# A fused attention and MLP kernel: first projections by row pieces of the q, k weights, products of chunk 0 in halves, weights of chunk 1 spread by SBUF to SBUF transfers

## The chip, the cores and the metric

The kernel runs on one core of one Trainium2 chip. The metric is the device time of one execution in microseconds (us); the time before is the median of three runs. One more execution was profiled, and all views are of that one.

## The reference, cut to what matters

```python
S, D, H, Dh, W, dil, F = 2048, 512, 32, 16, 8, 2, 1376      # batch 1, bf16

def attention(x, wqkv, wo):                                  # x: layernormed rows
    q, k, v = split(x @ wqkv)                                # 32 heads of 16 each
    idx = pos[:, None] - arange(W)[None, :] * dil            # 8 keys per row: 0, 2, ..., 14 rows back
    logits = einsum("bhsd,bhswd->bhsw", q, k[idx]) * Dh ** -0.5
    attn = softmax(where(idx >= 0, logits, -1e9))
    return einsum("bhsw,bhswd->bhsd", attn, v[idx]) @ wo

def mlp(x, W_gate, W_up, W_down):
    gate = relu(x @ W_gate)
    return (gate * (x @ W_up)) @ W_down

h  = x + attention(layernorm(x), wqkv, wo)
h2 = h + mlp(layernorm(h), W_gate, W_up, W_down)
```

## The kernel before

The 2048 rows are taken in four chunks of 512 (`tk` = 0 to 3). Each chunk passes through the same stages, and the stages of different chunks are interleaved.

1. **Layernorm and transposition.** DVE takes row statistics (L431, L434), ACT the reciprocal root (L444, L448), DVE writes the normed rows (L466). They are transposed by TensorE (L495) and copied out of PSUM by ACT or DVE (L511, L509), or, for those named in `DMAT`, by DMA transposes on SP's queue (L484). All of chunk 3's first layernorm goes by DMA (`xtd`).
2. **Projections.** Twelve of 512 columns each (L536): four each of q, k and v, every one of them four matmuls, one for each of four row blocks (`dt`) of the weights. ACT copies each out (L544). The first four of chunk 0 are run in two halves of the chunk's rows, 256 columns at a time.
3. **Scores.** DVE multiplies q by the shifted k (L583, `pr`), for four shifts and two of the four dimension groups at a time, 128x4096 elements in one instruction. TensorE sums over the head's dimensions (L589, `sc`), ACT takes the exponential (L619); in chunk 0 DVE masks the first columns (L622, `mk`). TensorE and ACT form one over the softmax sum (L639, L642, L645).
4. **Spreading the weights.** Each weight is needed in four partitions. In chunks 0 and 1 TensorE does that (L689, `bc`, two groups of four matmuls of 32x512 that run beside each other), and ACT copies eight results out (L695, `be`). In chunks 2 and 3 (`BCD`) eight transfers of 128 KB from SBUF to SBUF on SP's queue do it (L679, `bd`). In chunks 1 to 3 the weights are scaled by the reciprocal first (L663, `am`).
5. **Weights times v.** DVE multiplies (L710, `mu`, 128x4096, once for each of four dimension groups) and adds up eight products: first eight to four, by an accumulating DMA that GpSimd issues (L742, `ta`, 512 KB, chunks 0 to 2) or on DVE, then four to two and two to one on DVE (L713, L717, L736).
6. **Output projection and MLP.** L762 and L765 (`wo`), the residual (L771, L773), the second layernorm, the up and gate projections (L800), their copies on ACT (L804, L807), the product on DVE (L820), the down projection (L837, `dn`), the sum (L848) and the store (L854).

**What sets the order.** Each step is an `Op` with an engine, an expected duration, its dependencies and its buffers. `Plan.order` plays all of them through, with one queue for each engine that is sorted by the table `RANK`, and the program is written out in the order of the planned start times. So the order on each engine is fixed when the program is built, and an instruction that waits holds up all that stand behind it on its engine. The expected load times (`xload`, `wload`) and durations only shape that order and the choice of buffers; the chip waits for semaphores.

At the start each of SP's and ACT's queues issues two x row blocks and two row blocks of the q, k weights:

```python
for j in range(BPC):
    (nc.scalar if j % 2 else nc.sync).dma_start(x_sm[:, j:j + 1, :], x_rows[:, j:j + 1, :])
for dt in range(NT):
    (nc.scalar if dt % 2 else nc.sync).dma_start(wqk_sb[:, dt:dt + 1, :], w3_r[:, dt:dt + 1, 0:2 * D])
nc.sync.dma_start(x_sm[:, BPC:2 * BPC, :], x_rows[:, BPC:2 * BPC, :])
```

While they land, TensorE runs 44 matmuls of zeros (L385), and 16 more behind its first transposes (L393).

Of the kernel before, what the change touches and what calls it, by code (L numbers as in the profile page):

```python
# [18 lines left out]
    0, 1, 2, 3, 4, 5, 6, 7, 8, 9, 10, 11, 12, 13, 14, 15, 16, 18, 19, 21,  # L19
    24, 32, 27, 17, 20, 22, 25, 26, 30, 35, 36, 29, 34, 37, 39, 41, 43, 47, 23, 28,  # L20
    31, 33, 38, 45, 48, 42, 59, 65, 40, 51, 55, 46, 56, 60, 49, 52, 57, 73, 76, 61,
    79, 67, 72, 71, 74, 80, 106, 88, 95, 75, 96, 91, 104, 103, 93, 113, 119, 127, 70, 85,
    94, 98, 102, 172, 175, 185, 130, 134, 136, 149, 152, 105, 108, 110, 114, 111, 188, 197, 223, 226,
    231, 179, 190, 217, 221, 228, 171, 180, 208, 211, 219, 158, 169, 195, 207, 210, 245, 252, 236, 241,
    239, 244, 243, 249, 256, 260, 247, 253, 246, 250, 255, 261, 266, 269, 276, 281, 275, 279, 285, 278,
    283, 282, 286, 291, 310, 315, 326, 330, 293, 322, 314, 324, 348, 329, 361, 337, 345, 339, 342, 346,
    350, 365, 333, 358, 349, 354, 340, 352, 353, 356, 363, 323, 328, 316, 321, 302, 313, 308, 312, 332,
    364, 373, 366, 370, 306, 379, 369, 394, 405, 359, 393, 355, 380, 402, 404, 421, 442, 445, 395, 424,
    453, 574, 374, 413, 447, 450, 389, 409, 436, 473, 50, 53, 44, 62, 54, 64, 58, 63, 66, 69,
    77, 90, 78, 83, 92, 81, 87, 82, 86, 89, 118, 129, 157, 170, 124, 196, 164, 178, 97, 101,  # L30
    166, 182, 100, 116, 150, 159, 132, 186, 107, 176, 137, 156, 109, 126, 200, 213, 218, 237, 232, 240,
    251, 258, 262, 264, 274, 284, 287, 288, 296, 294, 292, 298, 300, 307, 305, 309, 303, 318, 327, 360,
    367, 311, 319, 341, 347, 336, 343, 372, 377, 325, 334, 368, 375, 382, 385, 384, 388, 381, 383, 386,
    398, 390, 392, 397, 400, 387, 396, 401, 403, 406, 407, 408, 411, 414, 417, 410, 418, 412, 419, 422,
    457, 467, 434, 484, 477, 480, 461, 481, 491, 472, 475, 429, 466, 449, 460, 441, 476, 478, 433, 435,
    454, 458, 446, 451, 439, 443, 462, 474, 503, 427, 431, 469, 486, 502, 505, 508, 493, 512, 465, 525,
    507, 518, 511, 521, 529, 497, 516, 504, 513, 520, 531, 552, 569, 572, 524, 541, 666, 707, 514, 533,
    537, 540, 536, 539, 580, 708, 112, 120, 99, 121, 68, 84, 115, 122, 125, 133, 144, 163, 147, 160,
    165, 142, 148, 135, 145, 161, 229, 234, 233, 242, 187, 202, 177, 199, 174, 183, 192, 194, 184, 189,
    206, 235, 212, 215, 181, 191, 193, 205, 214, 238, 289, 265, 297, 317, 248, 257, 290, 301, 331, 335,  # L40
    338, 357, 344, 362, 371, 415, 425, 456, 459, 423, 432, 464, 470, 430, 438, 468, 471, 391, 399, 448,
    455, 479, 483, 490, 495, 485, 492, 482, 488, 487, 489, 499, 501, 494, 496, 498, 506, 509, 515, 519,
    522, 526, 528, 527, 534, 517, 532, 596, 601, 562, 594, 565, 589, 558, 591, 604, 544, 553, 542, 551,
    555, 560, 548, 550, 570, 549, 557, 546, 556, 579, 583, 568, 573, 586, 599, 608, 609, 614, 571, 576,
    603, 611, 618, 617, 626, 613, 629, 588, 631, 606, 627, 632, 620, 624, 585, 616, 635, 639, 662, 668,
    672, 623, 641, 643, 677, 628, 636, 638, 675, 634, 637, 645, 647, 117, 141, 128, 139, 131, 140, 123,
    138, 143, 146, 155, 162, 153, 167, 168, 173, 151, 154, 204, 225, 254, 268, 273, 299, 259, 270, 209,
    227, 216, 220, 267, 280, 224, 230, 201, 222, 198, 203, 263, 272, 271, 277, 304, 295, 320, 376, 378,
    351, 416, 420, 426, 428, 437, 444, 440, 463, 452, 530, 535, 543, 561, 500, 510, 523, 566, 547, 554,
    564, 567, 538, 545, 559, 563, 593, 597, 575, 578, 577, 581, 582, 587, 600, 602, 590, 598, 584, 595,  # L50
    592, 605, 607, 610, 619, 622, 615, 625, 621, 633, 612, 630, 657, 689, 683, 687, 667, 673, 671, 680,
    692, 640, 656, 658, 660, 648, 654, 650, 661, 664, 676, 679, 644, 652, 678, 682, 655, 663, 684, 649,
    651, 653, 670, 642, 646, 665, 669, 674, 694, 696, 685, 693, 659, 690, 681, 686, 698, 691, 699, 688,
    697, 701, 710, 714, 717, 719, 705, 709, 711, 715, 695, 702, 704, 706, 700, 703, 712, 713, 716, 718,
    720, 721,
# [36 lines left out]
class Plan:  # L92
# [23 lines left out]
    def order(self):  # L116
# [14 lines left out]
        while left:  # L131
# [36 lines left out]
            op.start, op.done = t, t + op.dur + op.lat  # L168
            if op.dq:
                at = max(t + op.dur + op.dq[0], free.get("DQ", 0.0)) + op.dq[1]  # L170
                free["DQ"] = at
                op.done = at + op.lat
            free[op.eng] = t + op.dur
# [18 lines left out]
def kernel(  # L192
# [22 lines left out]
    BCD = {(2,0):"SSSS",(2,1):"SSSS",(3,0):"SSSS",(3,1):"SSSS"}  # L215
    PRE = ()
    NAB = 0
# [127 lines left out]
    DAL = 5.5  # L345
    TDD, TDL = 1.25, 1.5
# [13 lines left out]
    HG = ([[0, 1, 2, 3]],) * 4  # L360

# [12 lines left out]
    def load(t):  # L374
        return add(None, "LD", 0.0, None, lat=t)

    xload = [[load(t) for t in (3.5, 3.7, 4.1, 4.35)]] + [[load(t)] * BPC for t in (9.15, 13.2, 15.4)]
    wload = {n: load(t) for n, t in
             (("q", 7.78), ("k", 7.78), ("v", 10.6), ("o", 17.1), ("u", 20.5), ("g", 24.0), ("d", 28.5))}
# [139 lines left out]
    for tk in range(NCK):  # L519
# [10 lines left out]
        for n, (c, t) in enumerate(seq):  # L530
# [3 lines left out]
            def f_mm(lo=0, hi=CS, c=c, t=t, mm=mm, xnT=xnT):  # L534
                for dt in range(NT):
                    nc.tensor.matmul(mm.t[:, lo:hi], lhsT=wv_sb[:, dt, t:D:NT] if c == 2 else wqk_sb[:, dt, c * D + t:(c + 1) * D:NT],  # L536
                                     rhs=xnT.t[:, dt, lo:hi], start=(dt == 0), stop=(dt == NT - 1))
# [9 lines left out]
            if tk == 0 and n < 4:  # L547

                a = None
                for i, (lo, hi, evs) in enumerate(((0, 2 * P, xev[0:2]), (2 * P, CS, xev[2:]))):  # L550
                    a = add(("qk%s%d" % ("ac"[i], n), tk), "PE", 4 * MM * (hi - lo) / CS + 0.02,
                            lambda f=f_mm, lo=lo, hi=hi: f(lo, hi), evs + [wl, a, fills[-1]], pr - 5, take=[mm],
                            use=[xnT], lat=PEL if i == 1 else 0.0)
            else:
                a = add(("qkv%d" % n, tk), "PE", 4 * MM, f_mm, xev + [wl], pr, take=[mm], use=[xnT], lat=PEL)
# [13 lines left out]
        for hf in range(2):  # L569
            sc, ex = Buf(at_s), Buf(ex_s)  # L570
            scd, prd = [], []
            for t in range(0, NT, 2):
# [13 lines left out]
                def f_sc(t=t, sc=sc, pb=pb):  # L586
                    for u in range(2):
# [5 lines left out]
                a = add(("pr%d" % hf, tk), "DVE", D40, f_pr, [d[k] for k in (t, t + 1) for d in (qd, kd, kp)],  # L593
                        apr, take=[pb], use=[qT], lat=DL)
                prd.append((a, pb, f_sc))
            if (tk, hf) in PRE:
# [72 lines left out]
        for w0 in range(0, W, BCN):  # L669
            hf = w0 // 4  # L670
            if (tk, hf) in BCD:
                for eng, q in (("SP", nc.sync), ("ACT", nc.scalar), ("POOL", nc.gpsimd)):
# [4 lines left out]
                    def f_bd(ws=ws, q=q, w0=w0, ab=ab, ex=exs[hf]):  # L677
                        for w in ws:
# [3 lines left out]
                                   take=[ab], use=[exs[hf]], lat=0.77, dq=(0.75 - 0.5 * (len(ws) - 1), 0.5 * len(ws))))  # L682
# [19 lines left out]
        for t in range(NT):  # L702
# [13 lines left out]
            def f_om(t=t, mt=mt, rc=rc, OT=OT):  # L716
                V.tensor_tensor(out=OT.t[:, t, :], in0=mt.t[:, 0, :], in1=rc.t[:], op=ALU.mult)  # L717

            m = add(("mu%d" % t, tk), "DVE", D40, f_mu, abd + [vd[t], kdone.get(("v", tk - 1, t))], tpr,
                    take=[mt], use=[ab], lat=DL)  # L720
# [17 lines left out]
            for n, du in ((4, D20), (2, D10), (1, D2)):  # L738
                f = lambda n=n, mt=mt, f=f_a: f(n, mt)
                if n == 4 and (tk, t) in DACC:  # L740
                    def f_da(mt=mt):
                        nc.gpsimd.dma_start(mt.t[:, 0:4, :], mt.t[:, 4:8, :], accum_op=ALU.add)  # L742

                    m = add(("ta%d" % t, tk), "POOL", 1.0, f_da, [m], tpr, use=[mt], lat=1.1, dq=(0.75, 2.74))
                    continue
                if n == 1 and tk in EARLY:
                    oev[t] = add(("tree%d" % t, tk), "DVE", du, f_al, [m], tpr, take=[OT], use=[mt], lat=DL)
                else:
                    m = add(("tree%d" % t, tk), "DVE", du, f, [m], tpr, use=[mt], lat=0.11)
# [39 lines left out]
        for f0 in range(0, NFT, 2):  # L789
# [3 lines left out]
            for ft in fts:  # L793
# [4 lines left out]
                def f_mm(w_sb, mm, ft=ft, fs=fs, hnT=hnT):  # L798
                    for dt in range(NT):
                        nc.tensor.matmul(mm.t[:fs, :], lhsT=w_sb[:, dt, ft * P: ft * P + fs],  # L800
                                         rhs=hnT.t[:, dt, :], start=(dt == 0), stop=(dt == NT - 1))
# [4 lines left out]
                def f_ge(gm=gm, gr=gr, fs=fs, i=ft - f0):  # L806
                    nc.scalar.activation(out=gr.t[:fs, i, :], in_=gm.t[:fs, :], func=ACT.Relu)  # L807

                a = add(("mm%d" % (f0 // 2), tk), "PE", 4 * MM, lambda f=f_mm, um=um: f(wu_sb, um), hev + [wload["u"]], pr,
                        take=[um], use=[hnT], lat=PEL)  # L810
                b = add(("ue%d" % (f0 // 2), tk), "ACT", A5, f_ue, [a], pr - 200, take=[ub], use=[um], lat=AL)
                c = add(("mm%d" % (f0 // 2), tk), "PE", 4 * MM, lambda f=f_mm, gm=gm: f(wg_sb, gm), hev + [wload["g"]], pr,
                        take=[gm], use=[hnT], lat=PEL)
# [93 lines left out]
```

## Time and profile before

| what | us |
|---|---|
| median of three runs (lowest, highest) | 200.46 (199.8, 200.73) |
| the profiled execution | 201.23 |
| its span, first to last instruction | 199.5 |
| TensorE (PE) busy | 191.6 (96%) |
| VectorE (DVE) busy | 152.6 (77%) |
| ScalarE (ACT) busy | 115.0 (58%) |
| GpSimd (POOL) busy | 12.6 (6%) |

The span leaves out 1.73 us of the profiled execution, ahead of the first instruction and behind the last. PE is TensorE's matmuls, PEld its weight loads, which run beside them. A busy share is an average over the whole span; which engine sets the pace in a stretch has to be read from that stretch. The granted clock of TensorE was 1.00 in nearly all of the span.

### The profile page before, as it was taken

The numbers are of one execution on the slowest core, as the hardware profiler recorded it, in microseconds if no ns is written. First come the engines' busy times: TensorE is split into PE (matmuls) and PEld (weight loads), VectorE is DVE, ScalarE is ACT, GpSimd is POOL, SyncE is SP. The second block draws the span as 40 slices with busy tenths as digits, with TensorE's granted clock in tenths as the row PEclk, the third lists the DMA queues.
The fourth block names the chain that finished last, engine by engine and source line by source line (L and its number), as shares of the span: only waits on it lengthen the run. The fifth ranks groups of instructions, "written<-read, shape, count | busy, mean of one in ns | idle before, by whom it ended". The sixth has DMA issues, their size and how long they took to land.

```text
span 199.5 us, 2918 instructions
## 1 busy us (share of the span) xinstructions
PE 191.6 (96%) x1080; PEld 95.7 (48%) x1099; DVE 152.6 (77%) x239; ACT 115.0 (58%) x240; POOL 12.6 (6%) x28
## 2 busy tenths in 40 slices
PE   8599999999999999999999999999999999999994
PEld 8385445554445344444444444444444444444542
DVE  6669999999999999998899859999964423032332
ACT  3455899881999987663844557701439620456500
POOL 4000000330000004100113000000000000000000
PEclk9999999999999999999999999999999999999999
DMA  6959981897000008985269970140010130102022
GB/s 166 327 185 324 412 283 32 156 192 148 3 0 0 3 0 157 190 165 123 39 118 196 208 204 2 26 85 20 3 53 0 26 79 0 31 0 79 0 79 79
DMA packets 19981, 20.92 MB, mean 105 GB/s; under 512 B 8608, under 2 KB 16768, under 8 KB 19968
## 3 DMA queue, kind: packets, MB, share of 16 engines
q1 hardware_dynamic: 17520, 13.60, 23.0%
q0 software_dynamic: 1728, 6.29, 16.8%
q10 hardware_dynamic: 720, 0.85, 1.6%
q8 instruction: 8, 0.13, 0.3%
q14 instruction: 5, 0.04, 0.1%
HBM read 8.42 MB, written 2.10 MB: 53 GB/s over the span
## 4 chain that ended last, share of the span: by engine, by line
PE 91%; DMA 4%; ACT 2%; issue 1%; SPq 1%; DVE 0%
PE bank L800 37%; PE bank L536 21%; PE bank L837 19%; PE bank L762 7%; DMA wqk_sb<-in_A_wqkv_dram 4%; PE bank L589 3%; PE bank L495 2%; ACT big L695 1%; PE bank L639 1%; ACT quad L511 1%; PE bank L765 0%; SPq L292 0%; PE bank L689 0%; ACT quad L544 0%; SPq L294 0%
## 5 line engine op out<-in xcount | busy, mean ns | idle before, releaser
L800 PE MATMUL bank<-quad,wu_sb 128*128 128x512 bf16 (+1 forms) x170 | 42.7, 379 | 0.7 <-ACT quad L511 0.3
L800 PE MATMUL bank<-quad,wg_sb 128*128 128x512 bf16 (+1 forms) x173 | 41.6, 379 | 0.1
L837 PE MATMUL bank<-wd_sb,gT 128*128 128x512 bf16 (+3 forms) x184 | 39.4, 366 | 0.2
L807 ACT ACTIVATE gr<-bank 128x512 bf16<-128x512 f32 (+1 forms) x44 | 25.3, 601 | 23.3 <-PE bank L800 21.8
L804 ACT CAST up_sb<-bank 128x512 bf16<-128x512 f32 (+1 forms) x44 | 25.1, 588 | 23.2 <-PE bank L800 22.4
L710 DVE TENSOR_TENSOR big<-big,vT 128x4096 bf16<-128x4096 bf16 x16 | 36.1, 2290 | 0.8 <-DMA big<-ex 0.6
L583 DVE TENSOR_TENSOR big<-quad,kT 128x4096 bf16<-128x4096 bf16 x16 | 36.2, 2288 | 0.4 <-ACT quad L544 0.4
L536 PE MATMUL bank<-quad,wqk_sb 128*128 128x512 bf16 (+1 forms) x140 | 30.3, 356 | 2.1 <-DMA wqk_sb<-in_A_wqkv_dram 1.8
L820 DVE TENSOR_TENSOR gT<-gr,up_sb 128x1024 bf16<-128x1024 bf16 (+1 forms) x24 | 15.2, 646 | 20.5 <-ACT up_sb L804 10.4
L837 PEld LDWEIGHTS <-gT 128*128 128x128 bf16 (+1 forms) x187 | 18.2, 98 | 19.7
L800 PEld LDWEIGHTS <-wu_sb 128*128 128x128 bf16 (+1 forms) x176 | 17.5, 100 | 21.1 <-issue 1.3
L800 PEld LDWEIGHTS <-wg_sb 128*128 128x128 bf16 (+1 forms) x176 | 17.6, 100 | 20.5 <-issue 0.2
L536 PEld LDWEIGHTS <-wqk_sb 128*128 128x128 bf16 x144 | 15.5, 114 | 14.3 <-DMA wqk_sb<-in_A_wqkv_dram 2.3
L848 DVE TENSOR_TENSOR row<-x_sm,bank 128x512 bf16<-128x512 bf16 (+1 forms) x17 | 10.8, 653 | 10.6 <-PE bank L837 10.6
L713 DVE TENSOR_TENSOR big<-big 128x1024 bf16<-128x1024 bf16 (+2 forms) x24 | 17.2, 735 | 0.7 <-DMA big<-big 0.6
L742 POOL DMA_DIRECT2D big<-big x12 | 10.5, 872 | 86.8 <-DVE big L710 42.7
L536 PE MATMUL bank<-quad,wv_sb 128*128 128x512 bf16 x62 | 15.2, 380 | 0.1
L762 PE MATMUL bank<-wo_sb,quad 128*128 128x512 bf16 x63 | 15.2, 379 | 0.1
L466 DVE TENSOR_SCALAR row<-x_sm,mv,rs 128x512 bf16<-128x512 bf16 x32 | 11.6, 407 | 2.3 <-ACT rs L448 2.1
L431 DVE BATCH_NORM_STATS2 st<-x_sm 128x6 f32<-128x512 bf16 x16 | 10.5, 680 | 3.4 <-DMA x_sm<-in_A_x_dram 3.4
L420 ACT ACTIVATE row<-x_sm,mv 128x512 bf16<-128x512 bf16 x12 | 8.6, 723 | 5.0 <-DVE mv L412 5.0
L544 ACT CAST kT<-bank 128x512 bf16<-128x512 f32 x16 | 9.2, 592 | 3.4 <-PE bank L536 3.4
(68 smaller groups left out, 141.6 us busy)
## 6 DMA issues: line engine op xcount, KB each, us to landing
big<-big POOLq DMA_DIRECT2D x12, 512.0 KB, 5.5
big<-ex SPq DMA_DIRECT2D x16, 128.0 KB, 2.8
out_dram<-row SPq DMA_DIRECT2D x15, 128.0 KB, 1.8
x_sm<-in_A_x_dram SPq DMA_DIRECT2D x3, 512.0 KB, 6.4
wu_sb<-in_B_W_up_dram SPq DMA_DIRECT2D x1, 1376.0 KB, 9.7
wg_sb<-in_B_W_gate_dram SPq DMA_DIRECT2D x1, 1376.0 KB, 12.7
wd_sb<-in_B_W_down_dram SPq DMA_DIRECT2D x1, 1280.0 KB, 15.7
wqk_sb<-in_A_wqkv_dram ACTq DMA_DIRECT2D x2, 256.0 KB, 7.2
```

Of the source, the lines that this page charges most:

```text
L466: V.tensor_scalar(out=xn.t[:], in0=x, scalar1=mv.t[:, j, 0:1], scalar2=rs.t[:, j:j + 1], op0=ALU.add if residual else ALU.subtract, op1=AL ...
L536: nc.tensor.matmul(mm.t[:, lo:hi], lhsT=wv_sb[:, dt, t:D:NT] if c == 2 else wqk_sb[:, dt, c * D + t:(c + 1) * D:NT], rhs=xnT.t[:, dt, lo:h ...
L583: V.tensor_tensor(out=pb.t[:].rearrange("p (t w) s -> p t w s", t=2), in0=q4, in1=k4, op=ALU.mult)
L710: V.tensor_tensor(out=mt.t[:], in0=ab.t[:], in1=v8, op=ALU.mult)
L713: V.tensor_tensor(out=mt.t[:, 0:n, :], in0=mt.t[:, 0:n, :], in1=mt.t[:, n:2 * n, :], op=ALU.add)
L762: nc.tensor.matmul(od.t[:], lhsT=OT.t[:, t, j * P:(j + 1) * P], rhs=wo_sb[:, t, :], start=(t == 0), stop=(t == NT - 1 and tk not in RPE))
L800: nc.tensor.matmul(mm.t[:fs, :], lhsT=w_sb[:, dt, ft * P: ft * P + fs], rhs=hnT.t[:, dt, :], start=(dt == 0), stop=(dt == NT - 1))
L804: nc.scalar.copy(out=ub.t[:fs, i, :], in_=um.t[:fs, :])
L807: nc.scalar.activation(out=gr.t[:fs, i, :], in_=gm.t[:fs, :], func=ACT.Relu)
L820: V.tensor_tensor(out=gt.t[:fs, 0:n, :], in0=gr.t[:fs, 0:n, :], in1=ub.t[:fs, 0:n, :], op=ALU.mult)
L837: nc.tensor.matmul(od.t[:, c0:c1], lhsT=gts[ft].t[:fs, ft % 2, j * P:(j + 1) * P], rhs=wd_sb[:fs, ft, c0:c1], start=(ft == 0), stop=(ft == ...
L848: V.tensor_tensor(out=ob.t[:, c0:c1], in0=x_sm[:, tk * BPC + j, c0:c1], in1=od.t[:, c0:c1], op=ALU.add)
```

## The change

- **Row pieces.** The first four projections of chunk 0 are cut in three: the first two row blocks of the weights for the first 256 columns, the same for the second 256, and then the other two row blocks for all 512. A piece waits only for the row blocks that it reads. 16 matmuls of 256 columns take the place of 32, and 8 of 512 are added.
- **Halves.** In chunk 0 (`PRS`, `MUH`) each q*k product and each weight*v product is two instructions of 128x2048 in place of one of 128x4096. A half of q*k waits for one dimension group's q and k in place of two; a half of weight*v waits for four of the eight spread weights.
- **Spread by DMA.** `BCD` now names chunk 1 as well: its eight TensorE matmuls and eight ACT copies go, and SP issues eight SBUF to SBUF transfers.
- **Order.** `RANK` is a new table. `Plan.order` and the expected load times are changed too (later loads, a slower landing of SP's transfers beside an accumulating DMA). With these the fixed order of instructions on every engine is another one from the first microseconds on. On DVE, for example, the four q*k products of chunk 0's second half are followed by others than before; on SP the four DMA transposes of chunk 3's first layernorm stand behind normed rows that come later than before relative to GpSimd's first accumulating DMA, and the eight new transfers of chunk 1 stand between them and the transfers of chunk 2.

The initial loads and their issue are as they were. New switches that are left empty (`PRD`, `DAC2`, `HSP`) add nothing.

```diff
-    BCD = {(2,0):"SSSS",(2,1):"SSSS",(3,0):"SSSS",(3,1):"SSSS"}
+    BCD = {(1,0):"SSSS",(1,1):"SSSS",(2,0):"SSSS",(2,1):"SSSS",(3,0):"SSSS",(3,1):"SSSS"}
+    PRS, MUH = (0,), (0,)
...
-    xload = [[load(t) for t in (3.5, 3.7, 4.1, 4.35)]] + [[load(t)] * BPC for t in (9.15, 13.2, 15.4)]
+    xload = [[load(t) for t in (3.5, 3.7, 4.1, 4.35)]] + [[load(t)] * BPC for t in (10.8, 14.4, 17.8)]
     wload = {n: load(t) for n, t in
-             (("q", 7.78), ("k", 7.78), ("v", 10.6), ("o", 17.1), ("u", 20.5), ("g", 24.0), ("d", 28.5))}
+             (("q", 9.55), ("k", 9.55), ("ab", 8.1), ("v", 12.1), ("o", 19.2), ("u", 22.6), ("g", 26.1), ("d", 30.1))}
...
-            def f_mm(lo=0, hi=CS, c=c, t=t, mm=mm, xnT=xnT):
-                for dt in range(NT):
+            def f_mm(lo=0, hi=CS, d0=0, d1=NT, c=c, t=t, mm=mm, xnT=xnT):
+                for dt in range(d0, d1):
...
-                a = None
+                ab, done = [wload["ab"]], []
                 for i, (lo, hi, evs) in enumerate(((0, 2 * P, xev[0:2]), (2 * P, CS, xev[2:]))):
-                    a = add(("qk%s%d" % ("ac"[i], n), tk), "PE", 4 * MM * (hi - lo) / CS + 0.02,
-                            lambda f=f_mm, lo=lo, hi=hi: f(lo, hi), evs + [wl, a, fills[-1]], pr - 5, take=[mm],
-                            use=[xnT], lat=PEL if i == 1 else 0.0)
+                    done.append(add(("qk%s%d" % ("ac"[i], n), tk), "PE", 2 * MM * (hi - lo) / CS + 0.005,
+                                    lambda f=f_mm, lo=lo, hi=hi: f(lo, hi, 0, 2), evs + ab + done + [fills[-1]], pr - 5,
+                                    take=[mm], use=[xnT]))
+                a = add(("qkd%d" % n, tk), "PE", 2 * MM, lambda f=f_mm: f(0, CS, 2, NT), done + [wl], pr - 4.9, take=[mm],
+                        use=[xnT], lat=PEL)
...
+                if tk in PRS:
+                    def f_p1(u, t=t, hf=hf, pb=pb, qT=qT, s0=s0):
+                        kb = kT[:, t + u, PADL + s0 - 4 * hf * DIL: PADL + s0 - 4 * hf * DIL + CS]
...
+                    for u in range(2):
+                        a = add(("pr%d%s" % (hf, "ac"[u]), tk), "DVE", D20, lambda u=u, f=f_p1: f(u),
+                                [d[t + u] for d in (qd, kd, kp)], apr, take=[pb], use=[qT], lat=DL)
+                        prd.append((a, pb, f_sc if u else lambda: None))
...
+            if tk in MUH:
+                def f_m1(hf, t=t, ab=ab, mt=mt, s0=s0):
...
+                ms = [add(("mu%d%s" % (t, "ac"[hf]), tk), "DVE", D20, lambda hf=hf, f=f_m1: f(hf),
+                          [x for x in abd if x.key[0][2] == str(hf)] + vds, tpr, take=[mt], use=[ab], lat=DL) for hf in range(2)]
```

## The prediction

> **What bounds the kernel now.** I read the page first (busy times), then the chain of work that ended last, then the timeline of its start, then the windows.
>
> ```profile
> PE 191.6 (96%) x1080; PEld 95.7 (48%) x1099; DVE 152.6 (77%) x239; ACT 115.0 (58%) x240; POOL 12.6 (6%) x28
> ```
>
> ```profile
> 2.16 7.84 DMA wqk_sb<-in_A_wqkv_dram
> 10.00 0.04 issue
> 10.05 0.85 PE bank L536 x6
> 10.89 0.45 PE bank L495 x8
> 11.34 0.87 PE bank L536 x8
> 12.21 0.01 issue
> 12.22 1.94 PE bank L536 x16
> ...
> 21.96 0.98 PE bank L589 x16
> ```
>
> The chain is one DMA up to 10.0 us and then TensorE alone until 196.5 us; the last 3 us are the final sum and store. So the time is the moment at which PE starts its real work, plus the work, plus PE's waits. PE's timeline of the start:
>
> ```profile
> 8.66 0.41 PE L536 MATMUL bank<-quad,wqk_sb 128*128 128x256 bf16 x2 [0.85 <-DMA wqk_sb<-in_A_wqkv_dram]
> 10.05 0.85 PE L536 MATMUL bank<-quad,wqk_sb 128*128 128x256 bf16 x6 [0.98 <-DMA wqk_sb<-in_A_wqkv_dram]
> ```
>
> The first two row blocks of the weights are there at 8.6; PE runs two matmuls, then waits 0.98 us at the third row block with everything else behind it. The other two blocks land at 10.0. The windows (us; PE, PEld, DVE, ACT, POOL busy; clock; DMA):
>
> ```profile
> 20.00:40.00 20.00, 19.84 (x132) 9.87 (x133) 19.84 (x31) 18.41 (x36) 1.87 (x2) 1.00 0.73 219
> 40.00:60.00 20.00, 19.90 (x114) 9.53 (x115) 19.59 (x23) 14.53 (x34) 1.72 (x2) 1.00 0.45 85
> 60.00:80.00 20.00, 19.51 (x140) 9.03 (x141) 20.00 (x16) 17.57 (x36) 2.58 (x3) 1.00 0.22 42
> 80.00:100.00 20.00, 19.89 (x93) 9.23 (x94) 18.73 (x33) 11.47 (x26) 1.72 (x2) 1.00 0.64 130
> ```
>
> PE idles about 0.1 us in 20, except in 60 to 80 (0.49). DVE is as full as PE until 80 us, so up to there two engines set the pace, and a gain on PE lasts only as far as DVE comes along.
>
> **Step 1, row pieces.** A 256-column matmul costs 1.94/16 = 0.121 us in the chain, a 512-column one 0.216 (3.45/16 further down it). The four projections cost 32 x 0.121 = 3.87 before, 16 x 0.121 + 8 x 0.216 = 3.66 after: 0.2 less. The start is now set by the normed rows. The last two (L466) end at 8.35 before; the new order puts a copy ahead of the last on DVE and another ahead of one root on ACT, so I take 8.6. All four transpositions then go ahead of the projections: first halves at about 8.75 to 9.7. Second halves wait for the last copy (L511, 0.59 us) and run 9.75 to 10.7; rows two and three (10.0) are there by then, and 8 x 0.216 end at 12.45. Before, this point is at 14.16. PE is 1.7 us ahead.
>
> Most of that is not kept, because DVE's load has not moved:
>
> ```profile
> 11.15 0.69 DVE L431 BATCH_NORM_STATS2 st<-x_sm 128x6 f32<-128x512 bf16 x1 [2.80 <-DMA x_sm<-in_A_x_dram]
> ```
>
> DVE waits 2.80 us for chunk 1's rows in both kernels. From 11.15 the new order gives it chunk 1's statistics (before: until 14.43 with a copy of 0.32 that is now earlier and an overlap of 0.08, so until 14.03), and then, ahead of chunk 0's first score sum, four half products (1.13 each, below), two L431 (0.60), four L466 (0.32) and one L434 (0.09): 7.1 us, to 21.15. PE gets there after 8 projections (0.863 each) and four transpositions (0.23): 12.45 + 7.8 = 20.3. So PE waits 0.9 us and starts that sum at 21.3, against 21.96 in the chain. The same number of projections lies ahead of it before. **Gain kept: 0.65 us.**
>
> **Step 2, halves.** A 128x4096 product takes 2.20 us from start to start (65.30 to 71.91 for three); the nearest row for 128x2048 is L713, 1222 ns long, of which 0.09 overlap the next, as with the large one (2288 against 2.20): 1.13. Two halves cost 0.06 more than a whole; eight of them 0.5 us on DVE, of which 0.12 are in the sum above. The rest is covered by PE's lead only where PE doesn't wait for DVE. By the plain durations the extra would be 2 x 1222 - 2288 = 156 ns, or 1.25 us in all; I take the steps, and keep 1.25 as the upper bound. [...]
>
> Adding up DVE's rows in the new order, its last L717 of chunk 0 ends at about 51.2, against 52.18: DVE is then 1.0 us ahead, since some 0.3 to 0.4 us waits that it had at 14.4 and 42.7 are filled. New small waits of PE come out of the same sums: for the mask (L622) 0.1 us, for the last L717 0.1, for a PSUM bank 0.1. The adds of chunk 0 may land late, see the rivals: 0.2 (0 to 0.6). **Given back: 0.5 us.**
>
> **Step 3, chunk 1's weights by DMA.** PE loses two groups of L689: 0.33 us each in the chain ("24.79 0.33 PE bank L689 x4" is one of chunk 0's): **0.66 us gained**, since PE is the chain there. ACT loses 8 x 0.63 us, off the path. PE's stall of 0.44 us in 64 to 70 came from the h transposes' copies, with L689 behind them:
>
> ```profile
> 65.37 0.44 issue
> 65.81 1.02 ACT quad L511
> 66.83 1.96 ACT big L695 x4
> ```
>
> The new order puts two projections (1.73 us) behind the transposes while those copies run: **0.3 us gained**. SP issues eight more transfers. The rows for them are chunk 2's and 3's:
>
> ```profile
> big<-ex SPq DMA_DIRECT2D x16, 128.0 KB, 2.8
> ```
>
> With 0.65 between issues, the second four start at about 65.5, when the scaled weights are ready, and the last lands by 70.2. DVE needs it at some 71.3 (71.91 before, less DVE's lead). What hides it are three products (L583, 2.2 each) that stand between. The longest landing of these sixteen, 4.9 us, would make DVE 1.1 us late; nothing else is on the DMA engines then (DMA share 0.01 in 64 to 70), so I cost it at nothing. On SP nothing waits behind them until chunk 2's, 13 us later.
>
> **Sum.** -0.65 - 0.66 - 0.3 + 0.5 = -1.1 us: a span of 198.4 and a profiled execution of 200.1. The median stands 0.77 under the profiled execution: **199.4 us**. All upper bounds at once (halves 0.75 more, adds 0.4 more, a late spread 1.1) would make +1.15, 201.6; by the lower ones (the waits at nothing, 0.5, and 0.9 in place of 0.65 kept of step 1, if PE's wait there is shorter) -1.85, 198.6.
>
> **Rival A: the gain is taken back at 100 us (no change).** The chain from chunk 1's products over an add, the output projection and the h transposes by DMA to chunk 1's MLP had 0.1 us to spare before (transposes landing at 103.65, first use at 103.75). It moves with DVE's lead, 0.6 us at 71.9, not with PE's 1.1. PE would wait 0.5 us there, and as much where chunk 2's adds land: 200.0 to 200.9. For it: these transfers again stand beside an add. Against: other down projections can cover it, and the new order issues these transposes 2 us earlier.
>
> **Rival B: chunk 3's transposes starve (slower).** Before, three of the four land by 37.3, ahead of the first add's data. In the new order they are issued from about 34.0, 35.3, 36.5 and 38.4, and the add at 33.9 has its data under way from 35.4. The trace shows the two beside each other, first 37.2 to 40.0:
>
> ```profile
> q0 software_dynamic: 128, 0.52, 104.1%
> q1 hardware_dynamic: 103, 0.03, 7.3%
> ```
>
> The transpose (128 KB) moves about one small packet (0.03 MB over 103 of them, some 256 bytes, so 512 in all) for each 4 KB packet of the add: 103 of its 512 in 2.8 us. If that holds through all four adds (to 46.9), with 440 more in the hole behind the first, some 900 of 2048 packets are left, and the last lands at about 49.7. PE needs chunk 3's rows at about 45 (22 projections and the sums behind 21.3). It would idle 4.7 us: 200.46 - 1.1 + 4.7 = 204.1. It decides from a landing after 46.2 on. Against it stands the window behind, 40.0 to 41.0:
>
> ```profile
> q1 hardware_dynamic: 440, 0.10, 51.8%
> q0 software_dynamic: 33, 0.07, 40.1%
> ```
>
> Where one add ends, the waiting transpose goes through whole, and the next add starts late. Then all land by 42.6 and only the adds are later. [...]
>
> **Rival C: the pieces gain nothing** (the normed rows later than 8.6, or a piece waiting for all four row blocks): step 1 is capped by DVE anyway, so up to 0.9 us later costs nothing. It is no case of its own.
>
> **How the numbers follow.** The forecast (198.7 to 200.0) has 0.58, Rival A 0.24, Rival B 0.13 (its prices 202 to 204.5), a late spread or add with a loss of 0.5 to 1 us 0.05. About 0.5%, 1.0 us, is what a measurement can tell. Seven tenths of the forecast lie below 199.46: faster 0.41. The rest of it, Rival A and a little more: same 0.43. Rival B and the late spread: slower 0.16. The range leaves out B and the ends of the rest; below it goes to 198.4, since a median of three runs that lie 0.9 us apart (199.8 to 200.73) may itself be 0.2 off: 198.4 to 201.4.
>
> **What would show it.** Right: PE's first L536 by 9.0 without a stall at 10.0; the first score sum at about 21.3 with a wait for DVE ahead of it; no L689 in chunk 1; the stall at 65 gone; PE's last matmul 1.1 us earlier. Wrong: a PE wait of over 1 us behind 12 us, above all at chunk 3's first projection (B) or at chunk 1's first L800 (A).

## The result and the profile after

| | before | after |
|---|---|---|
| median of four runs each, us (lowest, highest) | 200.56 (199.8, 200.73) | 207.86 (206.75, 208.86) |
| ratio after to before, 95% interval | | 1.0368 (1.0327 to 1.041) |
| profiled execution, us | 201.23 | 207.18 |
| its span, us | 199.5 | 205.4 |

The changed kernel is 3.7% slower. The prediction was 199.4 us, in a range of 198.4 to 201.4; what happened is its Rival B (chunk 3's DMA transposes held up beside chunk 0's accumulating DMAs), at a higher price than was put on it. Ratios leave disturbed executions out, so one can differ a little from the quotient of the medians. The page's busy line and its row of granted clocks, in 40 slices of 5.1 us:

```profile
PE 194.3 (95%) x1064; PEld 95.7 (47%) x1083; DVE 153.6 (75%) x247; ACT 111.8 (54%) x232; POOL 12.8 (6%) x28
PEclk9999999996699999999999999999999999999999
```

PE is busy 2.7 us longer than before (191.6) although it has fewer matmuls, and idle 3.2 us longer (205.4 - 194.3 = 11.1 against 7.9). Both come from one place, the two slices in which the clock row falls to 6. PE's timeline at the start, and around that place:

```profile
8.40 0.40 PE L512 MATMUL bank<-identity,row 128*128 128x128 bf16 x4 [0.25 <-DVE row L483]
8.63 7.09 PE L553 MATMUL bank<-quad,wqk_sb 128*128 128x256 bf16 x39
...
20.26 1.05 PE L608 MATMUL bank<-big,sel 128*32 128x512 bf16 x16
...
42.05 1.89 PE L553 MATMUL bank<-quad,wqk_sb 128*128 128x512 bf16 x8
49.28 3.15 PE L553 MATMUL bank<-quad,wqk_sb 128*128 128x512 bf16 x7 [5.34 <-DMA quad<-row]
52.65 1.91 PE L553 MATMUL bank<-quad,wv_sb 128*128 128x512 bf16 x4 [0.22 <-issue]
```

The start is as hoped: the first projections run from 8.63 without a stall, and the first score sum of chunk 0 stands at 20.26, against 21.89 in the same view before. Then PE waits 5.34 us at chunk 3's first projection, and the seven matmuls behind take 3.15 us, 0.45 each instead of 0.216. The chain of waits names what it waited for:

```profile
34.75 2.27 DVE big L773 x2
37.34 1.36 DVE big L773 x2
38.71 10.44 DMA quad<-row
49.28 3.15 PE bank L553 x7
```

`quad<-row` is chunk 3's DMA transposes (L501 here). The fourth was issued from 38.7 on and landed 10.44 us later. The windows (PE, PEld, DVE, ACT, POOL busy; clock; DMA):

```profile
20.00:40.00 20.00, 19.79 (x129) 9.92 (x130) 20.00 (x36) 15.38 (x31) 2.85 (x3) 1.00 0.65 176
40.00:60.00 20.00, 14.43 (x67) 6.06 (x67) 14.29 (x17) 7.19 (x15) 0.86 (x1) 0.83 0.58 79
60.00:80.00 20.00, 19.84 (x147) 9.07 (x149) 18.41 (x18) 16.52 (x39) 0.00 (x0) 1.00 0.22 53
80.00:100.00 20.00, 19.95 (x93) 9.30 (x93) 19.98 (x29) 12.14 (x25) 3.44 (x4) 1.00 0.80 157
...
49.00:53.00 4.00, 3.50 (x8) 1.32 (x10) 2.54 (x7) 0.00 (x0) 0.00 (x0) 0.50 0.36 72
53.00:57.00 4.00, 4.00 (x16) 1.72 (x14) 0.89 (x2) 1.40 (x3) 0.00 (x0) 0.79 0.00 0
```

Nearly everything is lost between 40 and 60 us. The clock is 0.50 in the 4 us behind the wait and 0.79 in the next 4, and VectorE, which was full there before (19.59), now waits as well: 14.29. Behind 60 us the kernel runs as before, some 6 us late. What the DMA engines did in 43 to 45, and then in 45.5 to 48.5 (queue, packets, MB, share of 16 engines; q0 carries GpSimd's accumulating transfers, "the adds", q1 the transposes):

```profile
q0 software_dynamic: 89, 0.35, 96.1%
q1 hardware_dynamic: 97, 0.02, 9.1%
...
q0 software_dynamic: 44, 0.15, 87.1%
q1 hardware_dynamic: 189, 0.04, 7.4%
```

In the first window a transpose moves one 256-byte packet for each 4 KB packet of an add, 97 in 2 us out of its 544: the prediction's first row, once more. In the second hardly anything moves: 0.19 MB in 3 us, while these packets take 94.5% (87.1 + 7.4) of the 16 engines' time. So the transposes issued between 33.3 and 41.6 landed at 38.7, 40.9, 43.3 and 49.1, the adds beside them at 38.1, 42.8, 48.6 and 51.1. Before, the transposes had landed at 34.7, 36.1, 37.3 and 41.5.

### The profile page after: what moved, and what is told of

The parts are those of the page before. It is cut to its first block, busy times and chain, and to the rows that moved or that the text cites. A ratio compares the mean times of both kernels' runs of the same rounds, so it can differ in the third digit from the quotient of the medians.

```text
span 205.4 us, 2921 instructions
## 1 busy us (share of the span) xinstructions
PE 194.3 (95%) x1064; PEld 95.7 (47%) x1083; DVE 153.6 (75%) x247; ACT 111.8 (54%) x232; POOL 12.8 (6%) x28
## 3 DMA queue, kind: packets, MB, share of 16 engines
q0 software_dynamic: 1728, 6.29, 18.2%
## 4 chain that ended last, share of the span: by engine, by line
PE 57%; DVE 23%; DMA 15%; issue 3%; DVEq 0%; POOL 0%
PE bank L865 28%; PE bank L910 14%; DMA quad<-row 7%; PE bank L553 7%; DMA x_sm<-in_A_x_dram 6%; PE bank L827 5%; DVE big L617 4%; DVE big L773 3%; DVE big L758 3%; DVE row L483 3%; DVE big L602 2%; DVE st L448 2%; PE bank L608 2%; DVE gT L893 1%; DMA big<-ex 1%
## 5 line engine op out<-in xcount | busy, mean ns | idle before, releaser
L865 PE MATMUL bank<-quad,wg_sb 128*128 128x512 bf16 (+1 forms) x172 | 42.5, 379 | 0.5 <-DMA quad<-row 0.3
L865 PE MATMUL bank<-quad,wu_sb 128*128 128x512 bf16 (+1 forms) x172 | 42.0, 379 | 0.2
L910 PE MATMUL bank<-wd_sb,gT 128*128 128x512 bf16 (+3 forms) x183 | 40.0, 366 | 0.2
L553 PE MATMUL bank<-quad,wqk_sb 128*128 128x512 bf16 (+1 forms) x132 | 31.3, 381 | 5.5 <-DMA quad<-row 5.3
L869 ACT CAST up_sb<-bank 128x512 bf16<-128x512 f32 (+1 forms) x44 | 24.4, 592 | 17.9 <-PE bank L865 13.2
L602 DVE TENSOR_TENSOR big<-quad,kT 128x4096 bf16<-128x4096 bf16 x12 | 27.2, 2284 | 3.7 <-ACT kT L561 3.5
L758 DVE TENSOR_TENSOR big<-big,vT 128x4096 bf16<-128x4096 bf16 x12 | 27.0, 2283 | 0.4 <-issue 0.4
L865 PEld LDWEIGHTS <-wg_sb 128*128 128x128 bf16 (+1 forms) x176 | 17.4, 100 | 21.1 <-DMA quad<-row 0.7
L865 PEld LDWEIGHTS <-wu_sb 128*128 128x128 bf16 (+1 forms) x176 | 17.5, 100 | 20.6 <-issue 0.4
L553 PE MATMUL bank<-quad,wv_sb 128*128 128x512 bf16 x62 | 16.7, 396 | 0.3 <-issue 0.2
L801 POOL DMA_DIRECT2D big<-big x12 | 10.6, 882 | 92.9 <-DVE big L758 62.9
```

What stands on the lines that cost most here:

```text
L602: V.tensor_tensor(out=pb.t[:].rearrange("p (t w) s -> p t w s", t=2), in0=q4, in1=k4, op=ALU.mult)
L758: V.tensor_tensor(out=mt.t[:], in0=ab.t[:], in1=v8, op=ALU.mult)
L865: nc.tensor.matmul(mm.t[:fs, lo:hi], lhsT=w_sb[:, dt, ft * P: ft * P + fs], rhs=hnT.t[:, dt, lo:hi], start=(dt == 0), stop=(dt == NT - 1))
L869: nc.scalar.copy(out=ub.t[:fs, i, :], in_=um.t[:fs, :])
L910: nc.tensor.matmul(od.t[:, c0:c1], lhsT=gts[ft].t[:fs, ft % 2, j * P:(j + 1) * P], rhs=wd_sb[:fs, ft, c0:c1], start=(ft == 0), stop=(ft == ...
```

## The experiments

The theory after the result: the new order issues chunk 3's transposes beside chunk 0's adds, and that alone costs the time. The rivals: the halves, the pieces or the spread cost it themselves; or most of it is the slow clock behind the wait and not the wait. All times are medians, and a ratio is to runs of the kernel before on the same chip: 200.77 us for early_x3, x3_pe, keep_warm and half_packets, 200.32 for the four kernels whose names begin with b_, 200.67 for late_x3, two_kb, early_norows and early_whole.

**early_x3: the changed kernel, and the order alone undone at one place.** VectorE takes chunk 3's statistics and normed rows (and chunk 2's normed rows, with ACT's root for chunk 3 and TensorE's transpositions of chunk 2) ahead of chunk 0's first weight*v product, so that three transposes are issued before the first add (34.73) and the fourth, at 35.28, before the first add's data move (36.3).

```diff
  RANK, places on DVE:
-  ... xxn2 xxn2 mu3c xxn2 xag3 xag3 xag3 mu3a xxn2 xxn3 xxn3 mu2a xxn3 mu2c mu1a xxn3 ...
+  ... xag3 xag3 xag3 xag3 xxn2 xxn2 xxn2 xxn2 xxn3 xxn3 xxn3 xxn3 mu3c mu3a mu2a mu2c mu1a ...
```

> The changed kernel with its order alone touched: on DVE and ACT chunk 3's statistics, roots and normed rows stand ahead of chunk 0's weight*v products, so that the four DMA transposes are issued before the first accumulating DMA. No work is added or left out. Theory 1 (the transposes starve beside the adds, and TensorE's clock falls in the wait): the 5.3 us wait at chunk 3's first projection goes, the clock stays at 1.00, and the time is 198 to 200.5 us. Theory 2 (the new order of products and projections itself is what costs, and the wait would turn up elsewhere): 205 us or more. Theory 3 (the loss comes from the eight new transfers of chunk 1 or the halves): about 207, as they are all still there.

Measured: 200.33 (199.99 to 200.9), ratio 0.998 (0.9963 to 0.9997). The transposes are issued at 31.3 to 36.5 and land at 33.8, 35.1, 36.4 and 40.6. The listing of DMA issues in 30 to 50 us (KB of one, median us from issue to landing), the changed kernel ahead, this one behind:

```profile
big<-big POOLq DMA_DIRECT2D x4, 512.0 KB, 7.9
quad<-row SPq DMA_TRANSPOSE x4, 6.1
```

```profile
big<-big POOLq DMA_DIRECT2D x4, 512.0 KB, 6.3
quad<-row SPq DMA_TRANSPOSE x4, 2.5
```

All of the loss (7.3 us) is gone, with pieces, halves and spread still in. The median is 0.2% below the kernel before, less than the 0.5% that the prediction calls measurable.

**x3_pe: the changed kernel with chunk 3's rows transposed by TensorE, so that no transpose stands beside the adds.**

```diff
-    DMAT = (('h',2,0),('h',2,2),('x',3,0),('x',3,2),('h',3,0),('h',3,2),('h',1,0))
+    DMAT = (('h',2,0),('h',2,2),('h',3,0),('h',3,2),('h',1,0))
```

> The changed kernel with chunk 3's first transposes done by TensorE (four of 0.23 us) and ACT (two copies of about 1 us) in place of DMA; the adds and everything else as they are. Theory 1: no wait for a transfer at chunk 3, 198.5 to 201 us, 0.5 to 1 us above the version that only moves them. Theory 2 and theory 3: 205 us or more.

Measured: 200.61 (200.14 to 201.29), ratio 1.0 (0.9985 to 1.0015). The loss is gone here too, with the changed kernel's order of normed rows and adds kept. TensorE does 16 transpositions and ACT two copies more; against early_x3 the intervals overlap.

**late_x3: the kernel before, with only this put in.** None of the change's parts is in it; on VectorE three of chunk 3's normed rows come behind chunk 0's first product with v, where one stood before (so two move, and not three as the expectation says).

```diff
  RANK, places on DVE:
-  ... xxn3 xxn3 xxn3 mu3 xxn3 mu2 ...
+  ... xxn3 mu3 xxn3 xxn3 xxn3 mu2 ...
```

> The kernel before, whole, with one thing moved: on VectorE three of chunk 3's four normed rows come behind chunk 0's first product with v instead of ahead of it, so that three of the four transposes are issued beside the adds (at about 36 to 39 us) and not ahead of them. None of the three parts of the change is in it. Theory (the loss comes from these transposes beside the adds alone): the last lands at 46 to 48 us, PE waits 3.5 to 5 us at chunk 3's first projection (42.8 us before), its clock falls behind the wait, and the median is 204 to 207. Rival (the loss of the changed kernel needs the halves, the pieces or the spread): the transposes land by 43, and the median is 200 to 201.5.

Measured: 205.27 (204.11 to 205.71), ratio 1.0221 (1.0185 to 1.0257). Three transposes land at 40.6, 42.7 and 45.3. PE's timeline, and the window behind its wait:

```profile
45.40 3.48 PE L536 MATMUL bank<-quad,wv_sb 128*128 128x512 bf16 x8 [3.30 <-DMA quad<-row]
...
44.00:48.00 4.00, 2.60 (x7) 1.06 (x8) 4.00 (x6) 0.79 (x2) 0.00 (x0) 0.69 1.07 207
```

Three instructions in other places turn the kernel before into one that is 4.6 us slower: a wait of 3.30 us and 1.75 us for eight slow matmuls (3.48 against 8 x 0.216). The wait is a little below what was expected, since the last transpose landed at 45.3 and not at 46 to 48.

**keep_warm: the changed kernel with 90 matmuls of zeros ahead of chunk 3's first projection**, whose results nothing uses, to keep the clock up through the wait.

```diff
+                for _ in range(90):
+                    nc.tensor.matmul(keep.t[:, 0:P], lhsT=warm[:], rhs=warm[:], start=True, stop=True)
```

> The changed kernel with 90 matmuls of zeros (128 columns, 0.056 us each, 5.0 us in all) put on TensorE just ahead of chunk 3's first projection, where it waits 5.3 us. The wait stays. If the fall of the granted clock behind the wait (0.50 in 49 to 53 us) is a cost of its own, it goes, and the time is 2 to 2.5 us less than the changed kernel's: 205 to 206 us. If the stretch behind the wait is slow for another reason (DVE, buffers), the time stays at 207.5 to 208.5.

Measured: 207.03 (206.04 to 210.05), ratio 1.0307 (1.0267 to 1.0348). Its window of 49 to 53, and its longest wait of PE:

```profile
49.00:53.00 4.00, 3.69 (x24) 2.01 (x21) 2.50 (x6) 0.00 (x0) 0.00 (x0) 1.00 0.45 90
```

```profile
PE bank L873 <- DMA quad<-row: 1.9, 1, 1.9
```

The clock stays at 1.00 and PE is about 2 us earlier at 58 us (its first output projection at 55.96 against 58.20). But at chunk 1's first up and gate projections, at 109 us, it waits 1.85 us for chunk 1's transposes, which again stand beside an add; the changed kernel waits 0.25 us there. So of 2.2 us that the clock costs on the spot, 1.6 are taken back in the profiled executions (spans 204.8 and 205.4). By the ratios the kernel is 0.6% (1.2 us) faster than the changed one, and the two intervals overlap: the expectation of 2 to 2.5 us was too high, and the slow clock by itself explains a small part of the loss.

**half_packets: meant to halve the adds' packets; the edit took no hold.** The adds still moved in 1728 packets as in the changed kernel, so this is a second run of it.

> The changed kernel with each of chunk 0's four adds issued as two adds of half the rows' length, so that its packets are 2 KB in place of 4 KB; the bytes are the same. If the DMA engines take one packet of the transpose for each packet of the add, the transposes move twice as fast beside the adds, the last lands 2 to 4 us earlier, and the time is 203.5 to 206 us. If the transposes are held up by whole adds whatever their packets, the last lands at 49 us as before and the time is 207 to 209 us.

Measured: 208.36 (206.53 to 209.29), ratio 1.0379 (1.0323 to 1.0435), with the last transpose landing at 48.8. Nothing follows for the packets.

**two_kb: the same edit, in force.** Each of chunk 0's adds is two adds of half the width; the adds now move in 2304 packets.

```diff
-                    def f_da(mt=mt):
-                        nc.gpsimd.dma_start(mt.t[:, 0:4, :], mt.t[:, 4:8, :], accum_op=ALU.add)
+                    def f_da(mt=mt, ws=((0, 4),) if tk else ((0, 2), (2, 2))):
+                        for w, k in ws:
+                            nc.gpsimd.dma_start(mt.t[:, w:w + k, :], mt.t[:, w + 4:w + 4 + k, :], accum_op=ALU.add)
```

> The changed kernel, but each of chunk 0's four adds is issued as two adds of half the width, so its packets are of 2 KB instead of 4 KB (twice as many, the same bytes). Theory (a queue of transposes and the queue of adds take turns packet by packet, and one transpose or so goes through where an add ends): twice as many turns and eight ends of adds instead of four, so chunk 3's last transpose lands at 44 to 46 us instead of 49.1, PE's wait at chunk 3's first projection falls from 5.3 us to 0 to 2, and the median is 201 to 204. Rival (the adds hold the DMA engines by their bytes and time, whatever the packets): the last transpose lands at 48 to 50 and the median stays at 207 to 208.

Measured: 208.88 (208.76 to 210.07), ratio 1.0427 (1.0387 to 1.0467). The last transpose lands at 50.8, and PE waits 6.8 us. The expectation failed (the rival's 48 to 50 is passed too). The first two transposes do land earlier than in the changed kernel (37.7 and 40.3 against 38.7 and 40.9), the third later (44.4 against 43.3). From 46.5 to 49.5 this kernel comes nearly to a halt:

```profile
q0 software_dynamic: 74, 0.14, 138.3%
q1 hardware_dynamic: 131, 0.03, 95.1%
```

205 packets in 3 us take 233% of the 16 engines' time: single packets take 1 to 3 us, those of the transposes included (on average 0.90 us for one of the adds and 0.35 us for one of the transposes, which took 0.02 in the changed kernel's window of 45.5 to 48.5). Taking turns is therefore not all that holds the last transpose.

**The parts alone, in the order of the kernel before.** b_rows has the pieces, b_halves the halves, b_spread the spread, b_all the three together; every step that both kernels have keeps its old place.

```diff
 b_rows      +  ("ab", 7.0) and the three pieces;  RANK of before, third piece behind the second
 b_halves    +  PRS, MUH = (0,), (0,);  RANK of before, halves in the place of the whole
 b_spread    +  BCD (1,0), (1,1): "SSSS";  RANK of before, transfers in the place of the matmuls
 b_all       +  all three
```

> The kernel before with its own order and the row pieces alone: the first four projections in three pieces each, the pieces of the last two row blocks behind the other pieces. Theory 1 (the loss of the change lies in its new order; the parts are small gains or nothing): TensorE starts the pieces when the first two row blocks land and doesn't wait at the third; 0.3 to 1.0 us faster than before, that is 199.8 to 200.5 where before is 200.8. Theory 3 (a part itself costs): a part that is behind the loss makes this kernel 2 us slower or more.

> The kernel before with its own order and the halves alone: each of chunk 0's q*k and weight*v products as two instructions, one right behind the other. Theory 1: 0.5 us more on DVE, of which TensorE feels 0 to 0.5: 0 to 0.5 us slower than before (200.8 to 201.3). Theory 3: 2 us slower or more.

> The kernel before with its own order and chunk 1's spread by eight transfers alone. Theory 1: TensorE loses 0.66 us of work and its wait at 65 us shrinks, 0.4 to 1.0 us faster than before (199.8 to 200.4). Theory 3: 2 us slower or more.

> The kernel before with all three parts in its own order, the steps that replace others standing in their places. Chunk 3's transposes are ahead of the first add, as before. Theory 1: 0.5 to 1.5 us faster than before (199.3 to 200.3), with no wait at chunk 3's first projection. Theory 3: near 207.

| kernel | median us (lowest, highest) | ratio (95%) |
|---|---|---|
| b_rows | 201.38 (199.85, 203.21) | 1.0039 (1.0011 to 1.0067) |
| b_halves | 200.46 (199.79, 200.98) | 1.0006 (0.9988 to 1.0025) |
| b_spread | 201.98 (200.75, 202.62) | 1.0076 (1.0051 to 1.01) |
| b_all | 202.06 (201.11, 203.62) | 1.0084 (1.0047 to 1.0122) |

None of the parts costs anything like 7 us, and none gains in the old order. b_rows, b_spread and b_all were expected 0.3 to 1.5 us faster than before and are 0.4 to 0.8% slower, so these three expectations failed; b_halves is within its own, 0 to 0.5 us slower. The traces show waits on VectorE's side that can have taken the gain; no run takes them out in the old order, so this is argued and not shown. Of b_rows, PE's timeline, and of b_spread, VectorE's:

```profile
11.86 4.52 PE L536 MATMUL bank<-quad,wqk_sb 128*128 128x256 bf16 x24 [2.14 <-DVE quad L509]
```

```profile
72.42 4.49 DVE L709 TENSOR_TENSOR big<-big,vT 128x4096 bf16<-128x4096 bf16 x2 [1.59 <-DMA big<-ex]
```

The pieces' second half waits 2.14 us for a copy that stands, in the old order, behind statistics that wait up to 2.5 us for chunk 1's rows. The spread weights come 1.59 us after VectorE could use them.

**The parts in the new order: early_x3 without one.** early_norows runs the first projections uncut, early_whole has whole products in chunk 0.

```diff
 early_norows:  early_x3 with the first four projections in two halves over all four row blocks
 early_whole:   early_x3 with
-    PRS, MUH = (0,), (0,)
+    PRS, MUH = (), ()
```

> The variant early_x3 without the row pieces: the first four projections run each half over all four row blocks again. Step 1 of the prediction (0.65 us kept, the rest is lost at the wait for VectorE's first products): 0.65 slower than early_x3's 200.3, so 200.7 to 201.3. Rival (VectorE's wait for chunk 1's rows caps it altogether): no difference, 200.2 to 200.5. Second rival (the whole 1.7 us is kept): 201.8 to 202.2.

> The variant early_x3 without the halves: chunk 0's four q*k products and four weight*v products are whole again, each where its second half stood. Step 2 of the prediction (halves cost VectorE 0.5 us and give nothing): 0.5 faster than early_x3's 200.3, so 199.6 to 200.1. Rival (in the new order the halves let VectorE start a product when one of its two tiles is there, which the whole product has to wait for): 0.5 to 1.5 slower, 200.8 to 201.8, with a wait of PE of over 1 us at chunk 0's second score sum.

Measured: early_norows 200.44 (200.06 to 201.8), ratio 0.9998 (0.9979 to 1.0017); early_whole 200.78 (200.3 to 201.75), ratio 1.0006 (0.9988 to 1.0024). Both expectations failed: neither 0.65 us more without the pieces nor 0.5 us less without the halves shows. The intervals overlap with early_x3's, so the medians do not rank the three; the profiled executions differ at the first score sum: 20.30 in early_x3, 20.46 without the pieces, 21.41 without the halves. So the pieces are worth some 0.16 us there, near the 0.2 by which the prediction's sum makes the four projections shorter. VectorE's timeline shows what the halves do, early_whole ahead of early_x3:

```profile
12.96 0.30 DVE L450 BATCH_NORM_AGGREGATE mv<-st 128x2 f32<-128x6 f32 x3
14.32 0.69 DVE L447 BATCH_NORM_STATS2 st<-x_sm 128x6 f32<-128x512 bf16 x1 [1.06 <-DMA x_sm<-in_A_x_dram]
```

```profile
13.03 0.30 DVE L451 BATCH_NORM_AGGREGATE mv<-st 128x2 f32<-128x6 f32 x3
13.24 1.21 DVE L617 TENSOR_TENSOR big<-quad,kT 128x2048 bf16<-128x2048 bf16 x1
```

VectorE waits 1.06 us for the next chunk's rows, and a half product fits into that hole; a whole one can't be put there without its second tile. In early_whole PE waits 1.08 us for this product at chunk 0's first score sum (the rival had put the wait at the second).

## Why the prediction was wrong, step by step

**The failed step is the weighing of Rival B.** It was given a chance of 0.13, on the sentence that where one add ends, the waiting transpose goes through whole and the next add starts late, so that all land by 42.6. The window that this was read from (40 to 41 us) held a single transpose with 440 packets left, and in its first half the adds moved nothing (0.00 MB in 40.0 to 40.5): it shows what a hole lets through, not that the holes are enough for four, which have 2176. In the changed kernel the hole behind the first add, 37.5 to 38.5, shows this:

```profile
q1 hardware_dynamic: 849, 0.21, 113.1%
q0 software_dynamic: 9, 0.00, 0.5%
```

849 packets go through, which is one and a half transposes; then the next add, issued at 36.45, has its data under way, and the later holes pass some 420 and 390. The last transpose lands at 49.14 and not by 42.6, and PE waits 5.34 us for it. A row with one transpose waiting was read as a rule for four. The cause and the place that Rival B names, transposes beside the adds and a wait at chunk 3's first projection, are what happened.

**That Rival B's own numbers came so close is in part luck.** It put the last landing at 49.7 (49.14 measured) and PE's idle time at 4.7 (5.34). Its count had one hole of 440 packets and some 900 left at 46.9. In the trace three holes pass 1660, and at 46.0 only 51 of the 2176 are left. These take until 48.6, since packets are held in a way that the count did not have (last section). At the pace beside an add, 97 in 2 us, they would have taken about 1 us: an estimate of a landing near 47.6 and, with PE ready at 43.9, a wait of some 3.8 us. late_x3, which shows no held packets, waits 3.30.

**The price was too low as well** (204.1 against 207.9). Missing were the clock, which fell to 0.50 behind the wait (late_x3: 1.75 us on eight matmuls), and VectorE: with the last adds landing at 48.6 and 51.1 it waits 0.71 and 1.46 us for them and 3.11 us for projections that come late:

```profile
48.59 0.69 DVE L761 TENSOR_TENSOR big<-big 128x1024 bf16<-128x1024 bf16 x1 [0.71 <-DMA big<-big]
51.08 1.36 DVE L761 TENSOR_TENSOR big<-big 128x1024 bf16<-128x1024 bf16 x3 [1.46 <-DMA big<-big]
56.22 4.49 DVE L602 TENSOR_TENSOR big<-quad,kT 128x4096 bf16<-128x4096 bf16 x2 [3.11 <-ACT kT L561]
```

Much of the clock's part alone is taken back at 109 us (keep_warm), so the terms don't simply add. For the clock's fall the trace of the kernel before gave no price: no wait of PE there is longer than 1.0 us, and the clock is 1.00 behind each. In the changed kernel PE is idle for 5.34 us, and the clock is 0.50 in 49 to 53, 0.79 in 53 to 57 and 1.00 from 57 on. How long a wait has to be for such a fall no run shows: in b_all the clock falls behind 1.90 us idle (last section).

**Step 1** kept more than 0.65 us up to the first score sum (1.63, with no wait of 0.9 there), but not by the pieces, which are worth some 0.16 (early_norows). The rest is the halves in VectorE's new order (1.1, early_whole), and probably loads that happened to land early. Chunk 1's rows, taken as fixed at 11.15, landed at 9.5 in the changed kernel's profiled execution and at 10.6 in early_x3's; the last weight rows landed at 10.0 in the execution that was profiled before, 8.3 in the changed kernel's and 7.8 to 9.5 in the twelve others. The stall of 0.98 us that the pieces were to remove changes with the execution: with the first projections still in two halves in the old order it is nothing in b_halves, 0.52 us in b_spread and 0.87 in late_x3.

**Step 2** had the right cost and missed the gain. In early_x3 eight halves of each kind take 9.4 and 9.2 us, against 8 x 2.25 = 18.0 for eight wholes: 0.6 us, near the 0.5 forecast from steps and half of the 1.25 by plain durations. In the old order that leaves no trace in the time (1.0006); in the new one the halves fill a hole.

**Step 3** holds in the new order. The window of 60 to 80 of early_x3 against 19.51 before:

```profile
60.00:80.00 20.00, 20.00 (x139) 9.00 (x137) 20.00 (x15) 14.88 (x31) 2.59 (x3) 1.00 0.50 106
```

The stall at 65 is gone and VectorE does not wait for the spread. In the old order the cover of three L583 products was not enough: 1.59 us late, above the upper bound of 1.1.

**The sum.** With Rival B out of the way, early_x3's span is 198.3, 1.2 us below the profiled 199.5 and next to the forecast 198.4; its median gains only 0.4 us (0.2%), as the span before was that of an execution with late loads. The agreement of the spans is in part luck, then, and step 1's share of it came from another place than forecast. So even without the failed step the likeliest answer was "no measurable change", and not 199.4.

**Rival A** was small: 0.25 us of wait at chunk 1's first L865 in the changed kernel, 0.3 in early_x3, where 0.5 was forecast; in keep_warm, where PE comes 2 us earlier, it is 1.85.

## What to carry to other kernels

When a new order makes DMA transposes start beside large accumulating transfers, count their packets through to the last landing and compare with the moment of use: one window in which a single transfer slipped through is no reason to discount that count. Where a count and a single window disagree, spread the range over both, and add to the price what followed the long PE wait here: the clock of 0.50 and the work that is late behind it. Time that a change frees need not be kept in an order of the other engines that was not made for it: the same three parts lost 0.8% in the old order (b_all), and 0.2% is all that they gained in the new one (early_x3).

## What the hardware showed beyond expectation

- **Packets that are held.** In the changed kernel's adds 27 packets of 4 KB took 1 to 3.2 us each between 45 and 48.5 us (otherwise 0.34). The same shows in its repeat, in keep_warm and in two_kb, and again in keep_warm at 106 to 108, beside chunk 1's transposes; no such group shows in the other ten traces (in the kernel before none of 1536 packets is over 1 us). 387 of the last transpose's 544 packets had just gone through between 45 and 46, and 51 were left; by the estimate above it might have landed some 1.5 us earlier without the hold. What sets it off was not tried and stays open: late_x3 also has a transpose beside two queued adds and shows none of it (a packet of its adds takes 0.31 us on average over the whole span, as in the kernel before; 0.35 in the changed kernel).
- **In b_all the clock fell behind a wait of 1.90 us.** In the profiled execution PE works until 9.63 us, with 0.63 us of work in 9 to 11, and waits until 11.53; the clock falls to 0.69 and 0.50 in the windows behind:

```profile
11.00:13.00 2.00, 1.47 (x8) 1.17 (x9) 1.97 (x6) 0.00 (x0) 0.00 (x0) 0.69 0.53 163
13.00:15.00 2.00, 2.00 (x7) 0.76 (x6) 1.43 (x5) 0.58 (x1) 0.00 (x0) 0.50 1.21 380
```

The length of the wait does not settle it: behind the 2.14 us of b_rows, at the same place, the clock stays at 1.00 in 11 to 15, and its 24 matmuls behind the wait take 4.52 us in place of 6.84 for 27 here.

- **Initial loads land at different times in different executions**, up to 2.2 us apart for the same issue times (7.8 to 10.0 us for the last weight rows, in fourteen traces), in a kernel whose start waits for them.
